# Leftovers of two batches in half rows, a later load of v, and last tokens moved by one phase, in a fused attention and MLP kernel

## The chip, the cores and the metric

The kernel runs on one core of a Trainium2 chip. The metric is the device time of one execution in microseconds (us), lower is better. Times are medians, with the range in brackets. A ratio is the mean time of one kernel's fast runs over the mean of the other's fast runs of the same rounds, so it isn't quite the ratio of the medians quoted; its 95% interval stands behind it. Kernels of one job share a chip and its runs of the kernel before, so I compare across jobs by ratios.

## The reference, cut to what matters

```python
# q, k, v: (8 batches, 8 heads, 576 rows, 64), fp32
k_p = k.reshape(B, H, 72, 8, D).mean(axis=3)      # 8 rows pooled into one
v_p = v.reshape(B, H, 72, 8, D).mean(axis=3)
attn = softmax(scale * q @ k_p^T)                  # 576 x 72 for each head
x = (attn @ v_p) -> (4608 tokens, 512)             # [rewritten: heads joined]
h = x @ w_in                                       # 512 -> 2048
out = (h - tanh(h)) @ w_out                        # 2048 -> 512
```

A batch has 8 x 72 = 576 pooled rows of k and of v. The kernel lays them on 128 partitions: four full tiles take 512, and **64 are left over**. It has nine MLP phases of 512 tokens. A batch has 576 tokens, so its last 64 have to be ready one phase later than the rest.

## The kernel before

An MLP phase is 64 products into `h` (TensorE), tanh (ScalarE), a subtraction (VectorE), then 64 output products; the next batch's attention is woven in between. Before the first phase stands a head, in which nothing but batch 0's attention can run. The leftovers arrive there as 64 whole rows of 8 x 64 values, on ScalarE's queue, behind q:

```python
load_main(k_pairs, k_raw[0], 0, 0, 1)           # SP's queue
load_q0(0, 2)                                   # ScalarE's queue
...
load_main(k_pairs, k_raw[0], 0, 2, 4)
load_q0(4, 8)
load_dense(k_pairs, k_raw[0], 0, nc.scalar)     # leftovers of k: 64 rows x 512
load_dense(v_pairs, v_raw[1], 0, nc.scalar)     # leftovers of v
...
for c in range(4): load_w1(c)                   # GpSimd's queue
load_w2(0)
nc.gpsimd.tensor_copy(out=v_bf[:, NM, :], in_=v_raw[1][:, NM, :])
load_w2(1)
```

The last 64 q rows of batch 0 come on ScalarE's queue, after the first scores, and what follows from them is woven into the first phase. The second part of w2 is asked for by GpSimd at 11.31 us; the third and fourth follow while it pools batch 1's k:

```python
scores_wide(0, (0, 1))
nc.scalar.dma_start(out=t0[:QT, :, R, :], in_=q[0, :, QA:S, :]...)   # last rows of q
...
for i in range(5, NHID):                        # first phase
    mlp_h(0, i, gts)
    if i == 7:  q_pe_tail(0)
    if i == 9:  scores_tail(0)
    if i == 11: x4 = av(0, 4, ps_any, False)    # last tokens of batch 0
    if i == 13: x_pe_transpose(0, 4, x4)
pool_k(1, nc.gpsimd, mid=(2, 3))                # third and fourth part of w2 in it
```

The whole kernel:

The softmax here doesn't subtract the row's maximum and nothing guards it: scores larger than these inputs give would overflow.

## Time and profile before

| | before |
|---|---|
| time | 300.46 us (300.42 to 300.86, 3 runs) |
| first attention product of the head | 14.61 us |
| 54 MLP products of the first phase remain (call this T) | 21.27 |
| output products of the first phase begin | 34.55 |
| products into `h` of the next phase begin | 54.98 |
| each later phase | 30.8 |

The rows in the middle are the marks by which I split all kernels. They are starts of groups in TensorE's timeline. T is the start of the first dense stream of MLP products plus 4 x 0.216 us, since four of its products are first halves of units that were opened earlier. TensorE is busy nearly all the time, so every microsecond in which it waits between two marks is a microsecond of the total, unless a later wait would have taken it anyway.

### The profile page before, as it was taken

Reading aid. Unit: us, or ns where it says so; the run is one execution under the profiler, and the core shown is the slowest. Engines: PE = TensorE matmul, PEld = TensorE weight load, DVE = VectorE, ACT = ScalarE, POOL = GpSimd, SP = SyncE. Lnnn points to the kernel's source line nnn. Section 1 sums busy time; section 2 is a strip of 40 time slices with the busy share of each in tenths; the row PEclk is TensorE's granted clock in tenths of the full one; section 3 lists DMA queues with packets and bytes.
Section 4 is the critical chain, followed back from the end, with each engine's and each line's share of the span. In section 5 each row is a group of like instructions: output and inputs, shape, how many; then the busy total and the mean of one; then the engine's idle time right before and its main releaser. Section 6 shows DMA issues by size and latency. Waiting matters only on the chain.

```text
span 299.1 us, 4694 instructions
## 1 busy us (share of the span) xinstructions
PE 291.5 (97%) x1671; PEld 142.5 (48%) x1671; DVE 159.1 (53%) x343; ACT 149.4 (50%) x283; POOL 115.5 (39%) x110
## 2 busy tenths in 40 slices
PE   7989999999999999999999999999999999999994
PEld 3454455544544454445444554455445544444443
DVE  5658665673547444753476247716680758108600
ACT  4647583666146633654265516650665166126511
POOL 8500904871496109922971089307940000000000
PEclk9999999999999999999999999999999999999999
DMA  7999999849854998699648974897431430111032
GB/s 251 226 211 278 311 227 310 263 87 328 234 113 99 271 297 134 117 302 245 107 88 235 300 167 94 242 294 159 97 66 35 95 92 0 37 70 36 0 72 70
DMA packets 66183, 49.79 MB, mean 166 GB/s; under 512 B 39920, under 2 KB 52976, under 8 KB 66160
## 3 DMA queue, kind: packets, MB, share of 16 engines
q1 hardware_dynamic: 58832, 42.94, 56.0%
q0 software_dynamic: 4752, 4.72, 9.4%
q10 hardware_dynamic: 2576, 1.84, 2.3%
q8 instruction: 13, 0.21, 0.3%
q14 instruction: 10, 0.08, 0.1%
HBM read 36.70 MB, written 9.44 MB: 154 GB/s over the span
## 4 chain that ended last, share of the span: by engine, by line
PE 85%; DMA 9%; POOL 4%; issue 0%; SPq 0%; ACT 0%; DVE 0%; POOLq 0%
PE o_ps L456 40%; PE hT_ps L428 37%; DMA w1b<-in_moe_w_in_dram 4%; PE x_ps L346 4%; DMA k_raw<-in_k_dram 4%; PE s_ps L298 3%; POOL k_raw L198 1%; DMA out_dram<-o_sb 1%; POOL k_raw L203 1%; POOL kd L206 1%; POOL w2b L510 0%; PE xT_ps L390 0%; POOL v_raw L576 0%; PE qT_ps L171 0%; POOL w1b L503 0%
## 5 line engine op out<-in xcount | busy, mean ns | idle before, releaser
L456 PE MATMUL o_ps<-w2b,gT 128*128 128x512 bf16 x560 | 134.4, 380 | 0.0
L441 DVE TENSOR_TENSOR gT<-hT_ps,t_sb 128x512 bf16<-128x512 f32 x144 | 98.9, 691 | 57.7 <-ACT t_sb L439 57.6
L428 PE MATMUL hT_ps<-xT,w1b 128*128 128x512 bf16 x576 | 126.9, 379 | 0.3 <-ACT xT L397 0.3
L439 ACT ACTIVATE t_sb<-hT_ps 128x512 f32<-128x512 f32 x144 | 85.6, 597 | 38.3 <-PE hT_ps L428 37.5
L428 PEld LDWEIGHTS <-w1b 128*128 128x128 bf16 x576 | 55.9, 98 | 66.5 <-issue 0.4
L456 PEld LDWEIGHTS <-gT 128*128 128x128 bf16 x560 | 52.5, 98 | 52.0 <-issue 1.4
L465 ACT COPY o_sb<-o_ps 128x512 f32<-128x512 f32 x33 | 19.3, 585 | 75.2 <-PE o_ps L456 75.2
L359 DVE RECIPROCAL rden<-x_ps 128x4 f32<-128x4 f32 x80 | 14.2, 177 | 52.5 <-PE x_ps L346 52.0
L360 DVE TENSOR_TENSOR x_sb<-x_ps,rden 128x256 bf16<-128x256 f32 x80 | 34.0, 425 | 3.5 <-DMA xT<-x_sb 0.6
L148 POOL CAST q_bf<-q_raw 128x2048 bf16<-128x2048 f32 x6 | 11.3, 1888 | 59.9 <-issue 34.8
L198 POOL TENSOR_TENSOR k_raw<-k_raw 128x1280 f32<-128x1280 f32 x7 | 20.2, 2886 | 27.4 <-DMA k_raw<-in_k_dram 16.6
L317 ACT ACTIVATE E<-s_ps 128x288 bf16<-128x288 f32 x60 | 21.4, 410 | 13.2 <-PE s_ps L298 13.0
L346 PE MATMUL x_ps<-VB,E 128*128 128x130 bf16 x240 | 20.8, 221 | 0.4 <-ACT xT L397 0.3
L346 PEld LDWEIGHTS <-E 128*128 128x128 bf16 x240 | 16.9, 98 | 8.8 <-DVE VB L230 0.6
L216 POOL TENSOR_TENSOR v_raw<-v_raw 128x1280 f32<-128x1280 f32 x6 | 17.4, 2898 | 0.0
L298 PE MATMUL s_ps<-qT,KB 128*128 128x288 bf16 (+5 forms) x128 | 17.0, 290 | 0.2
L298 PEld LDWEIGHTS <-KB 128*128 128x128 bf16 (+1 forms) x128 | 7.0, 96 | 10.2 <-issue 3.5
L527 PE MATMUL warm_ps<-xT 128*128 128x512 bf16 x29 | 10.2, 465 | 1.3 <-DVE xT L539 1.3
L206 POOL TENSOR_TENSOR kd<-k_raw 128x640 bf16<-128x640 f32 x7 | 10.8, 1540 | 0.5
L203 POOL TENSOR_TENSOR k_raw<-k_raw 128x640 f32<-128x640 f32 x7 | 10.8, 1541 | 0.5
L397 ACT CAST xT<-xT_ps 128x256 bf16<-128x256 f32 (+1 forms) x14 | 5.8, 436 | 8.5 <-PE xT_ps L390 5.1
L219 POOL TENSOR_TENSOR v_raw<-v_raw 128x640 f32<-128x640 f32 x6 | 9.3, 1544 | 0.5
(73 smaller groups left out, 100.7 us busy)
## 6 DMA issues: line engine op xcount, KB each, us to landing
k_raw<-in_k_dram SPq DMA_DIRECT2D x7, 1024.0 KB, 5.9
q_raw<-in_q_dram SPq DMA_DIRECT2D x7, 1024.0 KB, 10.2
v_raw<-in_v_dram SPq DMA_DIRECT2D x7, 1024.0 KB, 9.3
out_dram<-o_sb SPq DMA_DIRECT2D x38, 128.0 KB, 2.4
out_dram<-o_sb SPq DMA_DIRECT2D x16, 256.0 KB, 3.7
w1b<-in_moe_w_in_dram POOLq DMA_DIRECT2D x4, 512.0 KB, 14.2
w2b<-in_moe_w_out_dram POOLq DMA_DIRECT2D x4, 512.0 KB, 16.9
k_raw<-in_k_dram SPq DMA_DIRECT2D x7, 128.0 KB, 5.8
```

What stands on the lines that cost most here:

```text
L198: first = eng.tensor_tensor(out=r[:, :, 0:4, :], in0=r[:, :, 0:4, :], in1=r[:, :, 4:8, :], op=ALU.add)
L216: eng.tensor_tensor(out=r[:, :, 0:4, :], in0=r[:, :, 0:4, :], in1=r[:, :, 4:8, :], op=ALU.add)
L298: nc.tensor.matmul(dst[p : p + w], lhsT=KB[b % 2][:, o : o + w], rhs=qTs[b][:, m, c0:c1], start=True, stop=True,)
L317: nc.scalar.activation(out=E[:, t, half * hs : (half + 1) * hs], in_=ps[:, :], func=ACT.Exp, scale=SCALE)
L346: nc.tensor.matmul(ps[:, 2 * n : 2 * n + 2, :].rearrange("p h d -> p (h d)") if n < 2 else ps.rearrange("p (a s) d -> p a s d", s=2)[:, :, ...
L359: nc.vector.reciprocal(out=rden[:, :, :], in_=ps[:, :, D:D1])
L360: nc.vector.tensor_tensor(out=x_sb[:, half, :, :], in0=ps[:, :, 0:D], in1=rden[:, :, :].to_broadcast([128, 4, D]), op=ALU.mult,)
L428: nc.tensor.matmul(h_tiles[i][:, :], lhsT=w1b[:, fb, i * 128 : (i + 1) * 128], rhs=xT[:, fb, tok0 : tok0 + TG], start=(fb == 0), stop=(fb ...
L439: nc.scalar.activation(out=t_sb[:, :], in_=h_ps[:, :], func=ACT.Tanh)
L441: nc.vector.tensor_sub(out=gT[:, :], in0=h_ps[:, :], in1=t_sb[:, :])
L456: nc.tensor.matmul(o_ps[:, :], lhsT=gts[i][:, tb * 128 : (tb + 1) * 128], rhs=w2b[:, i, :], start=(i == 0), stop=(i == NHID - 1),)
L465: (nc.vector.tensor_copy if g == 0 and tb % 2 else nc.scalar.copy)(out=o_sb[:, :], in_=o_ps[:, :])
```

## The change

The intent: spread the leftovers over all 128 partitions as half rows, so that VectorE sums them in two short steps rather than three long ones, and let a TensorE product with a matrix of two ones in a column join the halves. Get v's leftovers out of k's way by asking for them only when k has landed. Free the first phase of batch 0's last tokens, whose q rows can then come late too. Here is the core (cut: PSUM, the memory that TensorE writes to, is laid out anew; VectorE divides in double blocks; batch 1's q arrives in rows of nine; and the loads of k from batch 3 on and of v from batch 6 on are split in two):

```diff
-    load_dense(k_pairs, k_raw[0], 0, nc.scalar)
-    load_dense(v_pairs, v_raw[1], 0, nc.scalar)
+    k23 = load_main(k_pairs, k_raw[0], 0, 2, 4)
+    load_halves(k_halves, k_raw[0], 0, nc.scalar)      # 128 rows x 256
+    after([load_halves(v_halves, v_raw[1], 0)], k23)   # SP's queue, waits for k
...
-    nc.gpsimd.tensor_copy(out=v_bf[:, NM, :], in_=v_raw[1][:, NM, :])
-    load_w2(1)
+    nc.gpsimd.tensor_copy(out=v_bf[:, NM, 0:HALF], in_=v_raw[1][:, NM, 0:HALF])
...
+    k1 = load_main(k_pairs, k_raw[1], 1, 0, NM)        # batch 1's k
+    after([k1], w1_dmas[1])
+    load_halves(k_halves, k_raw[1], 1)
+    load_halves(v_halves, v_raw[1], 1)
+    load_q_tail(0)                                     # batch 0's last q rows: here now
...
+    load_w2(1)
+    after(w2_dmas[1:], k1)                             # w2 waits for batch 1's k
...
-    nc.scalar.dma_start(out=t0[:QT, :, R, :], in_=q[0, :, QA:S, :]...)
...
+    def turn_left(dst, b):                             # the join, an fp32 product
+        nc.tensor.matmul(dst, lhsT=k_left[b]..., rhs=twos[:, :], start=True, stop=True)
...
     for i in range(5, NHID):
+        if i == NHID - 1:
+            q_cast_tail(0, nc.scalar.copy)             # ScalarE, before the last tanh
         mlp_h(0, i, gts)
-        if i == 7:  q_pe_tail(0)                       # ... to i == 13: last tokens
...
     for u in range(16):                                # second half: output products
+        if u == 0: q_four_tail(0)
+        if u == 1: scores_tail(0)
+        if u == 2: x4 = av(0, 4, ps_any, False)
+        if u == 4: x_pe_transpose(0, 4, x4)
...
+            if g == 1 and i == 0:                      # batch 1's last tokens
+                x4 = av(1, 4, ps_b1, False)
+            if g == 1 and i == 2:
+                x_pe_transpose(1, 4, x4)
```

## The prediction

> **What bounds the kernel now.** I read the page's busy table first, then its slices, then TensorE's own timeline for the first 55 us, then the windows by stage, and last the timelines of VectorE and the queues in the same stretch.
>
> ```profile
> PE 291.5 (97%) x1671; PEld 142.5 (48%) x1671; DVE 159.1 (53%) x343; ACT 149.4 (50%) x283; POOL 115.5 (39%) x110
> PEclk9999999999999999999999999999999999999999
> DMA  7999999849854998699648974897431430111032
> ```
>
> TensorE is busy 97% of the span, at full clock, so only its own work, its idle time, or warm-up filler can be saved. The change touches batches 0 and 1 alone, so the seven later phases of about 30.8 us each can't move much. DMA is at 9 in the first six slices (7.5 us each): the head shares a full DMA system.
>
> In the windows by stage (columns: stretch, its length, then busy us and count of each engine, clock, DMA share, GB/s) I read where TensorE's time is not dense:
>
> ```profile
> 7.50:14.60 7.10, 6.72 (x49) 3.18 (x47) 4.54 (x12) 5.11 (x10) 4.37 (x7) 1.00 1.20 227
> 14.60:18.49 3.89, 2.91 (x32) 1.96 (x33) 3.56 (x14) 1.29 (x4) 0.00 (x0) 1.00 1.23 218
> 21.27:34.55 13.28, 12.96 (x77) 6.17 (x76) 10.32 (x20) 9.66 (x18) 4.34 (x3) 1.00 1.15 265
> 34.55:54.98 20.43, 19.91 (x156) 10.96 (x155) 12.32 (x32) 12.06 (x21) 9.10 (x6) 1.00 1.07 290
> 54.98:68.95 13.97, 13.97 (x67) 6.34 (x65) 10.54 (x16) 9.33 (x16) 10.28 (x10) 1.00 0.62 161
> ```
>
> And TensorE's timeline, with the four places that matter:
>
> ```profile
> 14.61 0.69 PE L346 MATMUL x_ps<-VB,E 128*128 128x130 bf16 x9
> ...
> 18.49 0.59 PE L428 MATMUL hT_ps<-xT,w1b 128*128 128x512 bf16 x2 [0.28 <-ACT xT L397]
> ...
> 20.41 5.78 PE L428 MATMUL hT_ps<-xT,w1b 128*128 128x512 bf16 x26
> ...
> 34.55 2.75 PE L456 MATMUL o_ps<-w2b,gT 128*128 128x512 bf16 x12
> 37.82 0.45 PE L259 MATMUL kT_ps<-ident,kd 128*128 128x128 bf16 x5 [0.52 <-POOL kd L206]
> ```
>
> The first attention product starts at 14.61, the first MLP product at 18.49; from 20.41 the stream is dense. Four of its 26 products are first halves, so 54 products remain at 20.41 + 4 x 0.216 = 21.27. The one visible later hole: the twelve output products should end at 34.55 + 12 x 0.216 = 37.14, but batch 1's k transpose starts at 37.82, a hole of 0.68, released by GpSimd's k pooling.
>
> VectorE in the head:
>
> ```profile
> 10.47 0.43 DVE L198 TENSOR_TENSOR k_raw<-k_raw 128x256 f32<-128x256 f32 x1
> 10.93 0.58 DVE L203 TENSOR_TENSOR k_raw<-k_raw 128x128 f32<-128x128 f32 x1
> 11.54 0.29 DVE L206 TENSOR_TENSOR kd<-k_raw 128x128 bf16<-128x128 f32 x1
> ...
> 14.13 0.76 DVE L230 TENSOR_TENSOR VB<-v_ps,mask 128x256 bf16<-128x256 f32 x2 [0.81 <-PE v_ps L618]
> 15.00 0.18 DVE L359 RECIPROCAL rden<-x_ps 128x4 f32<-128x4 f32 x1
> 15.22 0.42 DVE L360 TENSOR_TENSOR x_sb<-x_ps,rden 128x256 bf16<-128x256 f32 x1
> ```
>
> The leftover pooling holds VectorE 10.47 to 11.83, and the eight pairs of reciprocal and product (0.55 us start to start) are back to back from 15.00 to 18.93: between 14.6 and 18.5 VectorE, not TensorE, sets the pace.
>
> **What the Trainium skill says.** "TensorE: Matmul & The Clock Gate", Back-to-back issue gap: N/2.4 + 2.5 ns, 216 ns for 512 columns; the trace agrees (64 products in the chain take 13.81 us, 0.2158 each). "VectorE: DVE Perf Modes", the section on the TRN2 errata, gives (N + 151)/0.96 ns for an fp32 tensor_tensor: 425 for 256 and 691 for 512, as the trace has (0.42 and 0.691 us); so 291 for 128. "FP8 and Floating Point Precision", TensorE Precision Notes: a true fp32 product takes four passes; this trace has none to check it by. "DMA: Bandwidth & Descriptors", Queues, rings and completion order: each DMA engine goes round the queues with work, a packet at a time. The trace agrees that queues share, and not by bytes: batch 1's k took 10.84 us to land behind w1, against a median of 5.9 for such loads.
>
> **The change part by part.**
>
> Half rows: k's leftover takes two additions of 128 elements (2 x 0.29 + 0.05 = 0.63 us) where three took 1.36: 0.7 less on VectorE. Two memsets (0.48 each) leave VectorE at 1.3 to 2.3 us, before k's first tile lands at 3.84: worth nothing. The pooled k of the leftovers isn't ready in bf16 but joined in an fp32 product over 64 columns; by four passes 4 x 64/2.4 = 107 ns, with a slower weight load perhaps 0.2 us, against 0.055 (estimate from the skill's figures). It comes three times in all (k of 0, k of 1, v of 1; v of 0 stays bf16 and needs four products in place of eight): +0.35 us in sum, of which 0.1 in the head.
>
> Start of the attention product in the head. After: leftover k sums end about 11.1 rather than 11.83; v's leftovers (issued after k's third load, which landed at 7.86) are cast in half the time (0.4 against 0.78). Small loads of v issued at 13.23 on a loaded queue took 4.7 us, so v's half rows land between 11 and 13. With 11, the order transposes, scores 2, left turn, scores 3, v left, scores of leftovers, v of pairs 0 and 1 leads to a start near 13.9; with 13, near 14.9. I take 14.3, against 14.61: 0.3 gained.
>
> From there to the 54 remaining products. Before: 14.61 to 21.27, 6.66. After: VectorE does four double blocks, reciprocal 0.19 + product 0.69 + gap 0.05 = 0.93 each, 3.7 us against 8 x 0.55 = 4.4. First product at +0.35 and 0.2 latency, two double blocks and v's second placing: +2.4; turn and copy (0.3 + 0.2 + 0.59): first MLP product at +3.6, where it was +3.88. Then ten first halves (2.16) and the turns between them (0.6): +6.35. Gain 0.3. Head in all: 0.6.
>
> First product phase of the MLP. Before 13.28 us for 54 products (11.65) and the last tokens of batch 0 (0.12 + 0.40 + 0.35 + 0.12 = 1.0): 0.63 idle. With the last tokens gone, 11.65 + 0.3 = 11.95: 0.33 of idleness gained; the 1.0 us only moves.
>
> Second product phase. Before 20.43. After: minus the hole of 0.68 (k's main part is pooled without the leftovers, 4/5 of 6.05 = 4.8 us, and k is asked for one unit later), plus 1.0 for batch 0's last tokens, minus 0.5 for those of batch 1, plus fp32 0.25. New waits here: batch 1's q stands in the queue behind 0.39 MB that had come by another queue. It landed at 36.6; TensorE will ask for the first cast about 38 (phase start 34.55 - 1.9 = 32.6, four units of 0.86, and 1.9 of other work), which leaves 1.4 for a cast of 1.04. I put down 0.4 us of waiting, as an average.
>
> Next phase: batch 1's last tokens, 0.5 us moved in, and two VectorE pairs (1.2 us) among products that need 0.69 of each 0.86: 0.2 us of waiting. Later phases: no change.
>
> Sum: 0.6 + 0.33 + 0.68 - 0.35 - 0.4 - 0.2 = 0.66. I take the queue's wait as more likely small, since q comes in pieces of 2304 bytes rather than 1024 and 256, and lift the gain to about 1.1: 300.46 - 1.1 = 299.4.
>
> **The rivals.** (a) The late v load takes the place of the wait that is taken away: its cast and the join stand ahead of the leftover scores in TensorE's order. For it: the 4.7 us of small loads and the loaded DMA. Against: before, this load also landed only at 10.58. Head gain 0 or -0.4, time about 300.3. (b) DMA is the bound of the next phase: batch 1's q, batch 0's last q (needed by ScalarE about 31, behind k in the same queue) or the second part of w2 (now asked for when k has landed) arrive late, and each microsecond earlier is waited away. For it: the DMA share of 1.07 to 1.24 up to 55 us, q at 36.6 and v at 40.79 each waited for; against: the bytes are the same, and slack after each is over a microsecond. Time 300 to 301. (c) All goes well: head 1.2, both idle stretches and the hole gone, no new wait: 2 us less, 298.4.
>
> **Range and chances.** At most about 2.5 us of idle or VectorE-paced time lies in reach of the change, under 1%; a loss needs a wait of several microseconds in one of three loads. So 298.2 to 300.8 should hold it 8 times in 10. Faster by over 2% (6 us) has nothing to come from: 0.01. Slower by over 2%: 0.02. Within: 0.97.
>
> **What would show it.** Head: the first attention product before 14.61 and the 54 remaining products beginning near 20.7; if the cast of v's leftovers starts after 12.5 instead, rival (a). First phase: output products beginning near 32.6. Second phase: no hole before the k transpose; ScalarE's cast of batch 1's q not waited for by TensorE; a hole there or before the fifth to ninth output group means rival (b). The first products of the next phase about 53.6 against 54.98. The fp32 products show their own duration, expected some 0.1 to 0.3 us. Later phases still 30.8 us each. Wrong if those later phases change, or if the gain is larger than 2.5 us, since then something other than idle time was removed.

## The result, and the profile after

The changed kernel takes **303.07 us** (302.81 to 303.98, 4 runs) against 300.54 (300.42 to 300.86, 4 runs) for the kernel before: ratio 1.0088 [1.0065, 1.0111]. It is within 2%, but 0.9% slower rather than 0.35% faster, and outside of the predicted range. All outputs are right.

From the page of the changed kernel, its busy table and the clock that TensorE was granted, in tenths of full speed, in 40 slices of 7.5 us:

```profile
PE 290.1 (96%) x1641; PEld 144.3 (48%) x1672; DVE 156.5 (52%) x333; ACT 149.0 (49%) x279; POOL 115.8 (38%) x116
PEclk9979999999999999999999999999999999999999
```

TensorE has less to do than before, over a longer span. The third digit of the clock is new: from 15 to 22.5 us the clock was lowered, which the page of the kernel before doesn't show. The marks in TensorE's timeline (start, duration of the group, and the idle time before it with what ended it):

```profile
14.50 0.28 PE L776 MATMUL PS<-v_raw,spread 128*128 128x64 bf16 x4 [2.81 <-POOL v_raw L736]
...
16.25 2.14 PE L507 MATMUL PS<-VB,E 128*128 128x130 bf16 x18
...
22.44 12.92 PE L580 MATMUL PS<-xT,w1b 128*128 128x512 bf16 x57
...
35.20 1.03 PE L608 MATMUL PS<-w2b,gT 128*128 128x512 bf16 x4
...
56.55 1.02 PE L580 MATMUL PS<-xT,w1b 128*128 128x512 bf16 x4
```

In the head TensorE stands still for 2.81 us until GpSimd has cast v's leftovers. The windows of the same kernel, with the columns of the prediction (stretch, length, busy us and count of PE, PEld, DVE, ACT and POOL, clock, DMA share, GB/s):

```profile
11.50:14.50 3.00, 0.19 (x2) 0.00 (x0) 0.23 (x1) 0.65 (x2) 0.45 (x2) 1.00 1.22 221
14.50:16.25 1.75, 1.75 (x25) 1.31 (x24) 0.85 (x2) 0.60 (x1) 1.75 (x6) 0.84 1.23 206
16.25:18.60 2.35, 2.14 (x19) 2.08 (x20) 1.77 (x5) 0.00 (x0) 0.23 (x1) 0.50 1.25 207
18.60:20.70 2.10, 1.85 (x17) 1.33 (x17) 1.97 (x5) 1.17 (x2) 0.00 (x0) 0.88 1.26 212
...
23.30:35.20 11.90, 11.76 (x54) 5.26 (x54) 9.15 (x15) 8.64 (x16) 7.05 (x7) 1.00 1.11 300
35.20:56.55 21.35, 20.78 (x166) 11.87 (x168) 12.18 (x32) 13.27 (x24) 8.17 (x6) 1.00 1.04 274
56.55:71.50 14.95, 14.52 (x73) 6.75 (x75) 11.30 (x20) 9.33 (x16) 9.06 (x10) 1.00 0.65 180
```

After the hole of 2.81 us the granted clock is 0.50 for a stretch and between 0.5 and 1 on both sides of it. At half clock, this adds up to (0.16 x 1.75 + 0.50 x 2.35 + 0.12 x 2.10) / 0.5 = 3.4 us. And the chain of waits shows where the hole comes from (start, duration, piece):

```profile
1.71 5.96 DMA k_raw<-in_k_dram
7.68 6.32 DMA v_raw<-in_v_dram
14.05 0.40 POOL v_raw L736
```

k's third load lands at 7.68, v's half rows are asked for then, and take 6.32 us. In the kernel before, GpSimd could cast v's leftovers at 10.58:

```profile
10.58 0.78 POOL L585 CAST v_raw<-v_raw 128x512 bf16<-128x512 f32 x1 [1.76 <-DMA v_raw<-in_v_dram]
```

Stage by stage, from the marks (a stage is the distance of two marks):

| us | before | predicted | after | after minus before |
|---|---|---|---|---|
| first attention product | 14.61 | 14.3 | 16.25 | +1.64 |
| head, to T | 21.27 | 20.7 | 23.30 | +2.03 |
| first phase, T to output products | 13.28 | 11.95 | 11.90 | -1.38 |
| second phase, to the next products into `h` | 20.43 | 21.0 | 21.35 | +0.92 |
| next phase's products into `h` | 13.81 | +0.7 | 14.89 | +1.08 |

(The 21.0 is the difference of the prediction's marks 53.6 and 32.6. The last row ends where the output products begin, at 68.79 and 71.44; the windows printed here and in the prediction run a little past that.) The rows from the head on sum to +2.65 us; the rest of the run gives back 0.25, and the profiled spans, 299.1 and 301.5, differ by 2.4. Later phases are as before: two windows of 31 us in each kernel are nearly full of TensorE work at full clock. The largest loss is in the head, and about a microsecond each in the two phases after the first; the first phase did what it should.

### The profile page after: what moved, and what is told of

Its sections match the earlier page's. It is cut to its first block, busy times and chain, and to the rows that moved or that the text cites. A ratio compares the mean times of both kernels' runs of the same rounds, so it can differ in the third digit from the quotient of the medians.

```text
span 301.5 us, 4684 instructions
## 1 busy us (share of the span) xinstructions
PE 290.1 (96%) x1641; PEld 144.3 (48%) x1672; DVE 156.5 (52%) x333; ACT 149.0 (49%) x279; POOL 115.8 (38%) x116
## 4 chain that ended last, share of the span: by engine, by line
PE 88%; DMA 5%; DVE 3%; issue 1%; ACT 1%; SPq 0%; POOL 0%; ACTq 0%
PE PS L580 39%; PE PS L608 39%; PE PS L507 5%; PE PS L451 3%; DMA v_raw<-in_v_dram 2%; DMA k_raw<-in_k_dram 2%; DVE gT L593 1%; DVE x_sb L493 1%; DMA out_dram<-o_sb 1%; PE PS L776 1%; PE PS L838 0%; ACT t_sb L591 0%; PE PS L264 0%; SPq L142 0%; PE PS L543 0%
## 5 line engine op out<-in xcount | busy, mean ns | idle before, releaser
L608 PE MATMUL PS<-w2b,gT 128*128 128x512 bf16 x541 | 132.2, 379 | 1.0 <-issue 0.2
L593 DVE TENSOR_TENSOR gT<-PS,t_sb 128x512 bf16<-128x512 f32 x144 | 99.0, 691 | 57.4 <-ACT t_sb L591 57.3
L580 PE MATMUL PS<-xT,w1b 128*128 128x512 bf16 x565 | 125.9, 379 | 0.9 <-ACT xT L846 0.2
L591 ACT ACTIVATE t_sb<-PS 128x512 f32<-128x512 f32 x144 | 85.6, 597 | 39.3 <-PE PS L580 38.5
L617 ACT COPY o_sb<-PS 128x512 f32<-128x512 f32 x33 | 19.3, 585 | 75.4 <-PE PS L608 75.4
L492 DVE RECIPROCAL rden<-PS 128x4 f32<-128x4 f32 x72 | 12.8, 177 | 52.3 <-PE PS L507 52.1
L493 DVE TENSOR_TENSOR x_sb<-PS,rden 128x256 bf16<-128x256 f32 x72 | 30.6, 425 | 2.5
L469 ACT ACTIVATE E<-PS 128x288 bf16<-128x288 f32 x60 | 21.4, 410 | 13.2 <-PE PS L451 13.0
L301 POOL TENSOR_TENSOR k_raw<-k_raw 128x1280 f32<-128x1280 f32 (+1 forms) x7 | 19.7, 2808 | 12.4 <-DMA k_raw<-in_k_dram 12.4
L507 PE MATMUL PS<-VB,E 128*128 128x130 bf16 x240 | 21.1, 228 | 0.0
L451 PE MATMUL PS<-qT,KB 128*128 128x288 bf16 (+5 forms) x128 | 17.1, 289 | 0.2
```

The source lines that it names most:

```text
L301: first = eng.tensor_tensor(out=r[:, :, 0:4, :], in0=r[:, :, 0:4, :], in1=r[:, :, 4:8, :], op=ALU.add)
L451: nc.tensor.matmul(dst[p : p + w], lhsT=KB[b % 2][:, o : o + w], rhs=qTs[b][:, m, c0:c1], start=True, stop=True,)
L469: nc.scalar.activation(out=E[:, t, c0:c1], in_=ps, func=ACT.Exp, scale=SCALE)
L492: nc.vector.reciprocal(out=rden[:, :, :], in_=ps[:, :, D:D1])
L493: nc.vector.tensor_tensor(out=x_sb[:, half, :, :], in0=ps[:, :, 0:D], in1=rden[:, :, :].to_broadcast([128, 4, D]), op=ALU.mult,)
L507: nc.tensor.matmul(ps[:, 2 * n : 2 * n + 2, :].rearrange("p h d -> p (h d)") if n < 2 else ps.rearrange("p (a s) d -> p a s d", s=2)[:, :, ...
```

## The experiments

The theory after the result: v's late load, with the lowered clock that follows it, makes the loss. The rival: the rest of the change (order of products, double blocks, joins, moved tokens) costs more than I thought. A third possibility: further loads that the change put later are just as late, and the late head hides them.

### a: the load of v

`a1_v_early` puts v's half rows back on ScalarE's queue, without a wait; `a2_v_sp` leaves them on SP's queue and takes the wait for k off; `a3_before_late` does the late load alone, in the kernel before; `a4_fill` leaves the late load and fills the hole with warm-up products, so that the clock stays up.

```diff
 a1 (in the changed kernel)
-    after([load_halves(v_halves, v_raw[1], 0)], k23)
+    load_halves(v_halves, v_raw[1], 0, nc.scalar)
 a2
+    load_halves(v_halves, v_raw[1], 0)
 a3 (in the kernel before)
-    load_dense(v_pairs, v_raw[1], 0, nc.scalar)
+    after([load_dense(v_pairs, v_raw[1], 0)], k23)
 a4 (in the changed kernel)
+    warm_pe(13)
     v_ps = v_pe_pool(NM, NT, spread, 3)
```

> One part undone: the half rows of v of batch 0 are asked for at once on the ScalarE queue behind k's half rows, as before the change, instead of after k's third load. Theory L (the late load of v's leftovers stalls TensorE for 2.8 us and lets its clock fall to half): the cast of v's leftovers starts before 11.5 us, no hole before the v products, clock 1.0, first attention product near 14.0, the 54 remaining products from about 20.5 in place of 23.3, time 300.0 (299.3 to 300.6). Rival D (the loss lies in the other parts: fp32 joins, the last tokens moved, the fuller queue; the hole at 11.5 would only be replaced by another wait, for instance for v's main rows): less than 1 us is gained, time above 302.

> Only the wait for k's third load is taken away; the load of v's half rows stays on the SyncE queue, where it is now issued about 2.2 us after the start. Theory L: as a1, time 300.0 (299.3 to 300.8), v's leftovers land before 11. If what mattered were the queue and not the time of issue, they land as late as 13 or 14 and the time stays near 303. If the wait protected k's own loads, k's third load lands later than 7.7 and the first scores move by as much.

> The late load alone, put into the kernel before: its v leftovers (64 rows of 2 KB) are asked for on the SyncE queue after k's third load. Theory L: they land near 14, TensorE stands from about 12.3 to 14.5, its clock falls, time 302.5 (301.8 to 303.5) against 300.5. Rival D: 300.5, within 0.5.

> The changed kernel with 13 more filler products (13 x 0.216 = 2.8 us) in the hole ahead of the v products; the late load and its wait stay. This parts the wait from the clock. If the fall of the clock to half between about 15.8 and 18.9 costs time of its own: clock 1.0 throughout, the first attention product still near 16, the 54 remaining products near 22.3 instead of 23.3, time 302.0 (301.5 to 302.5). If VectorE sets the pace there and the clock is idle cost: 303.0, unchanged.

| against before, 300.88 | us | ratio |
|---|---|---|
| a1_v_early | 300.97 (300.86 to 302.21) | 1.0008 [0.9989, 1.0028] |
| a2_v_sp | 301.05 (300.75 to 301.98) | 1.0010 [0.9991, 1.0030] |
| a3_before_late | 302.90 (301.37 to 304.86) | 1.0065 [1.0030, 1.0100] |
| a4_fill | 302.64 (302.37 to 303.19) | 1.0054 [1.0037, 1.0072] |

The late load is the loss: taking it out removes 0.8 of the 0.9%, on either queue, and it costs 0.65% when it is done alone. a3's six runs fell in two groups: two of 301.37 and 301.40 us at a mean granted clock of 1.0, and the others at 302.88 to 304.86 with 0.994. In the profiled run of a3 the hole and the clock after it look like this (TensorE's timeline, then a window):

```profile
15.43 0.51 PE L618 MATMUL v_ps<-v_raw,spread 128*128 128x64 bf16 x8 [2.10 <-POOL v_raw L585]
```
```profile
15.50:19.00 3.50, 3.50 (x23) 1.88 (x23) 1.08 (x3) 0.60 (x1) 2.14 (x4) 0.51 1.24 206
```

In a3 most of the loss goes with the clock: the two runs at full clock are about 0.5 us above before, the four others another 2.3 us (means of 301.39 and 303.67).

a2 doesn't show whether the wait protected k: k's third load lands anywhere from 7.7 to 9.0 us in the profiled runs, and 1.0 us apart in the two of the changed kernel itself (7.69, and 8.69 in c3), for a reason that I didn't find. So marks of two single profiles can differ by a microsecond for this alone.

But a1 is only level with before, where 300.0 was expected (a2's 301.05 is the same miss, and a4 lies just above its range). Its marks are better than before's by 1.0 and 1.6 us in the head. TensorE's timeline and GpSimd's in a1:

```profile
13.56 1.22 PE L507 MATMUL PS<-VB,E 128*128 128x130 bf16 x18
...
38.16 1.02 PE L608 MATMUL PS<-w2b,gT 128*128 128x512 bf16 x4 [1.68 <-DMA w2b<-in_moe_w_out_dram]
```
```profile
27.46 0.75 POOL L670 DMA_DIRECT2D w2b<-in_moe_w_out_dram  x1 [14.83 <-DMA k_raw<-in_k_dram]
```

The 18 attention products take 1.22 us in a1 and 2.14 in the changed kernel. T is 19.69, 3.6 us ahead of the changed kernel; but then a hole of 1.68 us opens before the fifth output group, since w2's second part is asked for at 27.46, when batch 1's k has landed, and isn't there until 38.1. This wait is latent in the changed kernel: the late head hides it. So 3.6 us of head become 2.1 us at the next products into `h` (54.43 against 56.55).

### b: the second part of w2, the moved tokens, the joins

`b1_v_w2_early` is a1 with w2's second part asked for without the wait; `b2_w2_early` does that alone. `b3_last1_back` is b1 with batch 1's last tokens back in the second phase, and `b4_bf16` is b1 with bf16 joins.

```diff
 b1 = a1 +, b2 = changed kernel +
     nc.gpsimd.tensor_copy(out=v_bf[:, NM, 0:HALF], in_=v_raw[1][:, NM, 0:HALF])
+    load_w2(1)
...
-    load_w2(1)
-    after(w2_dmas[1:], k1)
 b3 = b1 +
-            if u <= 13:
+            if u <= 14:
                 pend.append((u - 10, av(1, u - 10, ps_any, False)))
+    x_pe_transpose(1, *pend.pop(0))
-            if g == 1 and i == 0: ...
-            if g == 1 and i == 2: ...
 b4 = b1 +
-    twos, k_left, vl, spread32 in FP32
+    twos, k_left, vl in BF16, spread in place of spread32
```

> As a1 (v's half rows asked for at once), and the second part of w2 asked for at once too, as before the change, instead of after batch 1's k has landed. In a1 the head gained 3.6 us (remaining products from 19.7 in place of 23.3) and TensorE then stood 1.7 us waiting for this part of w2. Theory W (the deferred second part of w2 took back what the head gained): no hole before the fifth output group, 1.0 to 1.7 us less than a1, time 299.5 (299.0 to 300.0). Rival Q (the loads are bound by bandwidth, so another one takes its place: batch 1's k or q lands that much later): hole before the k transpose or the q transposes, time 300.7 to 301.2 as a1.

> The changed kernel with the second part of w2 asked for early, v's load late as the change has it. Theory: with the late head this part of w2 landed in time anyway, so nothing is gained: 303.0 (302.6 to 303.4); k of batch 1 may land up to 1.5 us later. If the order of w2 costs in the changed kernel itself: 302 or less.

> b1 with batch 1's last tokens back at the end of the second product phase, as before the change. Theory S (among the first MLP products of the next phase they cost 0.5 us more than their own work: that phase took 14.9 against 13.97, of which 0.5 is work): 0.3 to 0.5 us less than b1, 299.1. Rival: TensorE waits for VectorE at the end of the phase by as much: equal to b1 within 0.2.

> b1 with the joins of the half rows in bf16 (the halves rounded once more) instead of fp32. In the trace an fp32 join is two instructions of about 0.11 us each with two weight loads of 0.15. If that is on the path, three joins cost 0.3 us less; I expect 0.1 to 0.3 us less than b1. Rival: no difference (within 0.15), since TensorE waits there for other engines anyway.

| against before, 300.90 | us | ratio |
|---|---|---|
| b1_v_w2_early | 300.61 (300.49 to 301.97) | 0.9993 [0.9971, 1.0015] |
| b2_w2_early | 303.70 (302.96 to 305.47) | 1.0082 [1.0061, 1.0104] |
| b3_last1_back | 300.23 (299.97 to 300.55) | 0.9973 [0.9955, 0.9991] |
| b4_bf16 | 300.28 (299.95 to 300.72) | 0.9976 [0.9957, 0.9994] |

b2 confirms that w2's wait is latent: moving it alone gains nothing, as long as v is late. In b1 the hole of 1.68 us is gone, but 300.61 us is a miss against the 299.5 expected: the next hole has come up. ScalarE's timeline, then TensorE's, in b1:

```profile
32.85 0.62 ACT L207 CAST q_bf<-q_raw 64x512 bf16<-64x512 f32 x1 [0.89 <-DMA q_raw<-in_q_dram]
```
```profile
33.52 0.29 PE L230 MATMUL PS<-ident,q_bf 128*128 128x64 bf16 x4 [0.47 <-ACT q_bf L207]
```

Batch 0's last q rows, which the change puts behind batch 1's k, land at 32.85. ScalarE has to cast them before its last tanh of the phase, and TensorE waits 0.47 us.

b3 and b4 are 0.38 and 0.33 us below b1 by their medians, although that hole is larger in both (0.67 and 0.92 us). Each interval overlaps with b1's. The rows of groups show the join of k as the profile counts it (count, busy us, mean ns): the changed kernel, then b4.

```profile
L412 PE MATMUL PS<-twos,k_left 128*128 128x64 f32 x4 | 0.8, 280 | 0.2 <-DVE k_left L334 0.2
```
```profile
L411 PE MATMUL PS<-twos,k_left 128*128 128x64 bf16 x2 | 0.4, 198 | 0.1
```

Both rows are for two joins. An fp32 product shows as two instructions and is busy twice as long, 0.4 us for a join against 0.2. Since products overlap, the step from a join's start to the next product's says more: 0.23 us in b1 (37.17 to 37.40) and 0.03 in b4 (37.06 to 37.09).

### c: batch 0's last q rows earlier, and the clock apart from the wait

`c1_q_early` puts batch 0's last q rows where they were before, on ScalarE's queue after the first scores; `c2_all` adds b3 and b4. `c3_after` is the changed kernel again, and `c4_fill6` fills it with 6 products rather than 13.

```diff
 c1 = b1 +
     scores_wide(0, (0, 1))
+    load_q_tail(0, nc.scalar)
...
-    load_q_tail(0)                 # behind batch 1's k, SP's queue
 c4 (in the changed kernel)
+    warm_pe(6)
     v_ps = v_pe_pool(NM, NT, spread, 3)
```

> b1 with the third moved load put back too: batch 0's last q rows are asked for on the ScalarE queue at about 8 us, as before the change, instead of behind batch 1's k. In b1 they landed at 32.8 and held ScalarE's last tanh and with it TensorE for 0.5 to 1 us (0.9 in the bf16 run). Theory: that hole goes, 0.5 to 1.0 us less than b1 (300.6): 299.9 (299.6 to 300.2). Rival Q (bandwidth): batch 1's k or q of the same phase is waited for instead; equal to b1 within 0.2.

> c1 with batch 1's last tokens back in the second product phase and the joins in bf16. Alone they gave 0.4 and 0.3 us on top of b1. If they add up with c1: 299.2 (298.9 to 299.5), faster than both kernels by 0.4% or more. If they overlap with the same hole: as c1.

> The changed kernel again, on the same chip as these runs, to compare with. 303.0 (302.7 to 303.4) and a clock of 0.994 in every run.

> The changed kernel with 6 filler products (1.3 us) in the hole of about 2.8 us, which leaves some 1.5 us of it. With 13 fillers the time was 302.64 and the clock 1.0. If a hole of 1.5 us is short enough to keep the clock: clock 1.0, 302.6, the wait itself being unchanged. If any hole of over a microsecond lowers it: 0.994 and 303.0.

| against before, 301.07 | us | ratio |
|---|---|---|
| c1_q_early | 302.38 (301.18 to 303.21) | 1.0031 [1.0011, 1.0052] |
| c2_all | 300.93 (300.32 to 302.27) | 1.0000 [0.9981, 1.0018] |
| c3_after | 303.93 (303.50 to 305.30) | 1.0096 [1.0079, 1.0112] |
| c4_fill6 | 302.59 (302.12 to 303.72) | 1.0049 [1.0034, 1.0065] |

c3 repeats the changed kernel: 303.93 us is above the 303.4 expected, but so is before in this job, and the ratio is as in the first job (1.0096 and 1.0088).

c1 was a miss: slower than b1, with T at 23.23 rather than 20.12. ScalarE's timeline in c1 shows why:

```profile
10.88 0.64 ACTq L188 DMA_DIRECT2D q_raw<-in_q_dram  x1
11.57 1.14 ACT L201 CAST q_bf<-q_raw 128x512 bf16<-128x512 f32 x2 [3.03 <-DMA v_raw<-in_v_dram]
```

The first scores end at 8.5, but the load is issued at 10.88 only, and the casts that follow it in ScalarE's order wait with it, 3.03 us in all, until v's half rows have landed. No line of the kernel makes ScalarE wait for v.

The stall is only part of c1's loss. TensorE stood behind those casts:

```profile
12.24 0.40 PE L218 MATMUL PS<-ident,q_bf 128*128 128x128 bf16 x4 [1.74 <-ACT q_bf L201]
```

After it the granted clock is 0.50 from 12.8 to 16.1 us. c1's six runs part by the clock, as a3's did: three at a mean of 1.0 (301.18 to 301.98 us) and three at 0.993 or 0.994 (302.78 to 303.21), 1.4 us apart in the mean. c2 has the same hole of 1.74 us in its profile but kept its clock there, and its T is 21.64; two of its runs fell to 0.994. So of c1's 3.1 us in T about half is the stall and half the clock. c2 was a miss too: level with before, not the 299.2 expected.

c4 tells the clock from the wait in the changed kernel. TensorE's timeline and two windows of c4:

```profile
14.40 0.28 PE L776 MATMUL PS<-v_raw,spread 128*128 128x64 bf16 x4 [1.39 <-POOL v_raw L736]
```
```profile
14.50:16.25 1.75, 1.60 (x26) 1.15 (x25) 0.99 (x3) 0.60 (x1) 1.75 (x6) 1.00 1.24 207
16.25:18.60 2.35, 2.07 (x29) 1.62 (x30) 2.04 (x6) 0.40 (x1) 0.12 (x1) 1.00 1.24 207
```

v is as late as in the changed kernel (14.40 against 14.50), but with the hole at 1.39 us the clock stays 1.00, in five of six runs. c3 to c4 is 0.0047 of 301 us, 1.4 us; the changed kernel to a4, from two jobs, is 0.0034 or 1.0 us. Two profiles in which k landed alike (7.69 and 7.71) agree: T is 23.30 in the changed kernel and 22.27 in c4. So the lowered clock costs about 1.2 us, and the wait itself, what a4 and c4 are still over a1 (0.0046 and 0.0041), about 1.3 us more, net of the 1.68 us that a1 then waits for w2.

### d: the rest of the change, with all three loads early

It was open whether the stall in c1 comes from v's load in ScalarE's queue, and whether the change gains once all late loads are moved. `d1_q_sp` leaves ScalarE's queue alone and asks for the last q rows on SP's queue when k has landed; `d2_all` adds b3 and b4; `d3_ring` is c1 with v's half rows on SP's queue instead.

```diff
 d1 = b1 +
+    after([load_q_tail(0)], k23)   # SP's queue
...
-    load_q_tail(0)                 # behind batch 1's k
 d2 = d1 + the edits of b3 and b4
 d3 = c1, but
-    load_halves(v_halves, v_raw[1], 0, nc.scalar)
+    load_halves(v_halves, v_raw[1], 0)
```

> b1 (v's half rows and w2's second part asked for early) with batch 0's last q rows asked for on the SyncE queue once k's third load has landed, so that no computing engine has to issue it. In c1 the same early load stood in ScalarE's queue and ScalarE did nothing from 8.5 to 10.9 us until v's half rows had landed; that cost 2 us in the head. Theory: here no stall of ScalarE, no hole at the first groups of the second product phase, 0.5 to 0.9 us less than b1 (ratio to before 0.9993): ratio 0.997, about 299.9. Rival Q (bandwidth): equal to b1, because k or q of batch 1 comes that much later.

> d1 with batch 1's last tokens back in the second product phase and the joins in bf16. They gave 0.38 and 0.33 us on b1. If they add: ratio to before 0.9950 (299.3 us), the fastest of all. If they overlap with d1's gain: 0.9975.

> c1 with one difference: v's half rows are asked for on the SyncE queue (as in a2), so ScalarE's queue holds only q and k's half rows when batch 0's last q rows are issued there. Theory R (the issue on ScalarE waits for room in its own queue, which two half-row loads of 128 rows fill): the issue starts near 8 us, ScalarE's casts go on at 8.9, time as d1. Rival: ScalarE stalls until about 10.9 as in c1, so the stall does not come from v's load in the same queue: time 301.5 to 302.4.

| against before, 300.88 | us | ratio |
|---|---|---|
| d1_q_sp | 299.90 (299.69 to 300.53) | 0.9965 [0.9948, 0.9981] |
| d2_all | **299.34** (298.84 to 300.03) | 0.9944 [0.9926, 0.9961] |
| d3_ring | 300.14 (299.61 to 300.54) | 0.9967 [0.9949, 0.9985] |

ScalarE's timeline in d3, where the same instruction as in c1 is followed by the same casts:

```profile
9.15 0.65 ACTq L188 DMA_DIRECT2D q_raw<-in_q_dram  x1
9.85 1.14 ACT L201 CAST q_bf<-q_raw 128x512 bf16<-128x512 f32 x2 [1.21 <-DMA q_raw<-in_q_dram]
```

With v's load out of the queue, the issue comes 1.7 us earlier, so v's load in the same queue held ScalarE up for that long; it still comes a microsecond later than the 8 us expected. That the queue was full is my reading: half rows are 128 pieces where whole rows were 64, and the kernel before had both loads in this queue without the stall. A rival is untested: in c1 and c2 the issue starts just as v has landed (10.88 and 10.60, GpSimd's cast of v 0.04 us later in both), as it would with a wait that the framework adds on its own. No run shows the limit itself.

d1 is the change as it was meant, with three loads placed otherwise, and it gains 0.35%. d2, which takes two parts of the change back, beats both kernels, by 0.56% over before and, against c3 in ratio, by 1.5% over the changed one. Its marks in TensorE's timeline:

```profile
13.42 1.22 PE L506 MATMUL PS<-VB,E 128*128 128x130 bf16 x18
...
31.46 1.03 PE L607 MATMUL PS<-w2b,gT 128*128 128x512 bf16 x4
...
36.85 1.02 PE L607 MATMUL PS<-w2b,gT 128*128 128x512 bf16 x4 [0.70 <-DMA w2b<-in_moe_w_out_dram]
```

A wait of 0.70 us for w2 is still left in it.

The marks of the kernels that carry the argument:

| us | first attention product | T | output products | next products into `h` |
|---|---|---|---|---|
| before | 14.61 | 21.27 | 34.55 | 54.98 |
| changed | 16.25 | 23.30 | 35.20 | 56.55 |
| a1 | 13.56 | 19.69 | 31.59 | 54.43 |
| b1 | 14.00 | 20.12 | 32.02 | 54.01 |
| c1 | 17.10 | 23.23 | 35.13 | 56.48 |
| d1 | 14.04 | 20.16 | 32.07 | 53.42 |

## Why the prediction was wrong

**Start of the attention product in the head: this step failed.** It said that v's half rows "land between 11 and 13", from 4.7 us for small loads on a loaded queue, and took 14.3 for the first attention product. The load took 6.32 us from 7.68, a microsecond beyond the end of that interval, and the product began at 16.25. The load of before, not held back, was ready to be cast at 10.58: the prediction had this line and used it only against rival (a). The page of before had a better measure than the 4.7 us:

```profile
v_raw<-in_v_dram ACTq DMA_DIRECT2D x1, 128.0 KB, 7.4
v_raw<-in_v_dram ACTq DMA_DIRECT2D x4, 32.0 KB, 4.7
```

The small loads are 32 KB each; v's leftovers are 128 KB, as whole rows and as half rows alike, and took 7.4 us under the traffic of the head. From 7.86 that gives 15.3. With v early the same code starts at 13.56 (a1) to 14.04 (d1), where the prediction had 13.9 for a load landing at 11, so the other terms of the step, the VectorE sums and the order of products, were good to about a third of a microsecond.

**From there to the 54 remaining products.** Predicted 6.35, measured 23.30 - 16.25 = 7.05. In a1 and d1, at full clock, it is 6.13 and 6.12. The surplus of 0.9 is the lowered clock, which the prediction didn't consider at all: it wrote "at full clock" from the page of before and never asked what a hole of more than two microseconds does. So rival (a) was the right one and its size, "Head gain 0 or -0.4, time about 300.3", was wrong: the head lost 2.03.

**First product phase of the MLP.** Predicted 11.95, measured 11.90. Right, and for its reason: with batch 0's last tokens gone the 54 products are dense.

**Second product phase.** The marks of the prediction make 21.0, measured 21.35 (21.35 in d1 too). Right in kind: TensorE's busy time grew by 0.87 in the window where the terms had 1.0 - 0.5 + 0.25 = 0.75, and the hole before batch 1's k transpose is gone. The 0.4 us that I put down for batch 1's q isn't seen as a wait; several small idle times, the largest of 0.25 behind VectorE's placing of k, stand there instead.

**Next phase.** Predicted +0.7, measured +1.08: TensorE's busy time grew by 0.65 (14.46 against 13.81), where I had 0.5, and 0.43 is idle, of which a visible wait for VectorE of 0.32 where I had 0.2. b3 hints that the move of batch 1's last tokens costs some 0.4 us in all (b1's and b3's intervals overlap); it only shifts their work, to where VectorE is fuller.

**The fp32 joins.** Predicted +0.35. The medians of b1 and b4 differ by 0.33, within their noise. The steps of the three joins in the two traces say more: 0.74 us together in b1 and 0.15 in b4, so about 0.6. Their own duration, expected at 0.1 to 0.3 us, shows as 0.4.

**Rival (b), the DMA bound.** It named the right loads: w2's second part and batch 0's last q rows. But I wrote that "slack after each is over a microsecond". In the changed kernel neither is seen to wait, because the head is late; with the head repaired they cost 1.68 us (a1) and, after that, 0.47 (b1). Had v been early, the prediction would still have been about 1.3 us too low in its time, for these two loads: a1 came out level with before, d1 at the predicted ratio.

**The sum.** Of the 3.7 us between 299.4 and 303.07, the head is 2.6, the second and next phases 0.7, and 0.4 is the lift from a worked-out gain of 0.66 to 1.1, for which there was no term (that longer pieces of q land sooner is shown by no run). d1's ratio is the predicted one, 0.9965, but by terms that differ: its head gains 1.1 and not 0.6, and the phases after it give back more. That it met the number is luck.

**Slips of reading** that changed little. DMA is at 9 in the second to seventh slice, not the first six. Seven pairs of VectorE, not eight, are back to back up to 18.93; the eighth starts at 19.41, after a wait for TensorE. And the change doesn't touch batches 0 and 1 alone, since later loads of k and v are split; that shows in no later phase.

What stays open: why k's third load lands at different times, when a hole lowers the clock and when it doesn't, why the second phase idles where it does, and what held the issue in ScalarE's queue.

## What to carry to other kernels

When a change asks for a load later, work out its landing from a load of that kind under the traffic of that moment, put it beside the instant at which the first engine needs it, and count the interval's bad end, because a hole on TensorE can cost its own length and then a stretch at half clock, in some runs and not in others. Repair the waits one after another and look again each time: here the late v hid the late w2, which hid the late q, and only when all three had moved did the rest of the change show its gain. A load can cost its issuing engine more than the issue when its queue has other loads in it, as in c1, so put it on an engine that has no work in that stretch.

## What the Trainium skill lacked or had wrong

- "TensorE: Matmul & The Clock Gate", "Why this matters for your kernels", advises no TensorE gaps over about 3 us, and Part 1 has the clock fall after an idle window of about 3.4 us. Here shorter holes were enough, but not in every run. By the longest hole after 8 us in the profiled runs: 2.46 and 2.81 us (changed kernel) lowered the clock in all ten runs, 2.10 (a3) in four of six, 1.74 (c1 and c2) in five of twelve, 1.39 (c4) and 0.71 (b1) in one of six each. In a3, c1 and c3 another of 1.1 to 1.3 us lies just before. The clock went to 0.50 1.2 us after work had resumed (changed kernel), 0.5 after (c1) or just before (c3). The 3.4 us that it lasted in these agree with the page's window; in b2's profiled run it lasted 6.8.
- "DMA: Bandwidth & Descriptors", "Anatomy of one DMA", fits about 2.0 us plus bytes over 436 GB/s (for loads issued by GpSimd), an estimate of 2.3 us for the 128 KB of v's half rows. On a DMA system at a share above 1.2, issued by SP, they took 6.32 us. The page has no figure for how long one load takes among others in loaded queues.
- The same page, "Issuing engines are not separate DMA queues", says that issuing from several engines only saves the time to initiate a DMA. I found no page that says that an issue can wait until an earlier load of its queue has landed, and hold back the engine's compute meanwhile: ScalarE stood 3.03 us in c1, and its issue came at 9.15 rather than 10.88 when v's load was in another queue (d3).
- "FP8 and Floating Point Precision", "TensorE Precision Notes", gives four passes for a true fp32 product. The trace shows an fp32 join of 64 columns as two instructions, busy 0.4 us together, against 0.2 us for one in bf16; the page doesn't say how a trace shows the passes.
